# Table products with bf16 one-hots: a token's number as two bf16 parts, in place of one fp32 number

## The chip, the cores and the metric

The kernel runs on one core of one Trainium2 chip. The metric is the device time of one execution in microseconds (us). The engines are named as in the profile: PE (TensorE; PEld is its weight load), DVE (VectorE), ACT (ScalarE), POOL (GpSimd) and SP (SyncE, which here only issues transfers).

## The reference

A state-space scan (Mamba-2's SSD) for 4 batches, 8 heads, 768 steps, head size 32 and state size 16 gives 3072 rows of 256 numbers. A cosine router then sends every row to one of 8 experts, and the expert's two matrices turn the row. What matters here is the routing:

```python
logits = xn @ en.T / tau
expert_idx = np.argmax(logits, axis=1)
...
for e in range(E):
    mask = expert_idx == e
    h = np.maximum(x[mask] @ w1[e], 0.0)
    out[mask] = gate_w[mask, None] * (h @ w2[e])
```

The mask of an expert is, in the kernel, a table: for each expert and each place in it, the number of the token that stands there.

## The kernel before

**The scan.** `mamba` goes through the 768 steps in 6 chunks of 128 steps; a chunk has 4 units of 128 tokens, one per batch. In each chunk PE makes inner products (`inner`, L351), DVE masks them (`mask_inner`, `g`, L361), PE makes the outputs from the running states and the masked products (L372, L389, L402), turns them into rows (`finish`, L421), ACT copies the rows (L413, L430, L432) and SP sends them to a table of rows in DRAM, `y_rows` (`send_rows`, L436). The state goes from chunk to chunk through `decay_states` (`T` on DVE, L307, then `U` on POOL, L313) and `add_sums` (`V` on DVE, L336). `scale_c` makes `cp` on DVE (L243), `pass_c` scales a part of it on POOL (L256), and `scale_first_half` makes `xb` on POOL (L278).

**The routing.** It trails the scan by some chunks, in small steps between the scan's. `pick` (L533 to L539) makes for each token of a chunk a one-hot of its expert (`ob`, bf16). `count_picks` (POOL, L544) keeps running counts of the units. `rank_rows` (PE, L559) gives each token its rank within its expert, by products of bf16 matrices of ones, and ACT copies the ranks (L567). `places` (DVE, L578 to L603) splits a rank into a tile of 104 places and the place within the tile. It makes two one-hots: `eq`, over 8 experts x 4 tiles, and `hot`, over the 104 places. `eq` is multiplied by the token's number plus 1 (`tok1`). `locate` (PE, L613) multiplies the two for each of the 4 units of the chunk, `hot` as the weights and `eq` as the moving operand: the result, 104 places x 32 tiles, holds the number of the token at each place, plus 1.

```python
        k.nc.tensor.matmul(
            k.pz[0][:TR, 424 : 424 + E * NT], lhsT=hot[:, b, :],
            rhs=eq[:].rearrange("p (b e) t -> p b (e t)", b=NB)[:, b], start=(first and b == 0),
```

ACT copies this table out of PSUM (L624) and POOL adds it up (L629).

**Where the calls stand.** The order on each engine is the order of the program; nothing reorders it. `places` of chunks 0, 1, 2 and 3 is called at the end of chunks 2, 3, 4 and 5, that of chunk 4 and 5 in `scan_end`. `locate` of chunks 0 and 1 is called in chunks 3 and 4, ahead of the second half of `finish`; that of chunk 2 in `early_places` in chunk 5, where DVE completes an early table `gi0` (L860, L862) from the first three chunks. With it POOL gathers the first rows of experts 0 and 1 (L876), PE turns them (L970), and the copy of the turned rows (L973) releases held weight loads (L84, L91) and a held send of rows. `locate` of chunks 3, 4 and 5 is called in `scan_end`, between the matmuls of the first expert (L983, L1000). `end_places` (L636 to L646) makes the full table `gi` and the rows of the output. From it come the gathers of all other rows. Those gathers wait for the sends of the last chunks' rows too.

**The experts.** `moe` runs through the 8 experts: `up` (L983), `down` (L1000, or L1045 with fewer products), `out` (L1085 to L1088), with gathers, weight loads and gates (`Gates`) beside them. `moe_end` is the end.

**Constants.** `route_consts` makes the number tables on POOL with `ints`: an iota (L494) and a cast to fp32 (L496) each.

Of the kernel before, what the change touches and what calls it, by code (L numbers as in the profile page):

```python
# [8 lines left out]
F32 = mybir.dt.float32  # L9
I32 = mybir.dt.int32  # L10
BF16 = mybir.dt.bfloat16
ACT = mybir.ActivationFunctionType
ALU = mybir.AluOpType
# [3 lines left out]
NB, NH, S, D, N = 4, 8, 768, 32, 16  # L17
Q = 128
HQ, SQ = Q // 2, Q // 4
NC = S // Q  # L20
NU = NB * NC
T = NB * S
DM, E, F = NH * D, 8, 1024
KD, KF = DM // 128, F // 128
TR, NT = 104, 4
# [23 lines left out]
def load(k, c):  # L49
    nc = k.nc  # L50
    t = k.ld[c]

    def in_(name, shape):
        return k.inp.tile([128] + shape, F32, name=name, tag=name)

    t.ct, t.bi, t.b = in_("ct", [NB, Q]), in_("bi", [NB, Q]), in_("b", [NB, 128])
    t.x, t.xa = in_("x", [NB, DM]), in_("xa", [NB, 128])
    def whole(dst, src):
        nc.sync.dma_start(dst[:].rearrange("p b m -> p (b m)"), src[c])

    whole(t.ct, k.CT)
    if c < 2:
        whole(t.bi, k.BT)
    whole(t.x, k.x)
    nc.sync.dma_start(t.xa[HQ:, :, :], k.x[c, 0:HQ, :].rearrange("p (b m) -> p b m", b=NB)[:, :, 128:])
    whole(t.b, k.B)
    if c >= 2:
        whole(t.bi, k.BT)
# [109 lines left out]
def spread_decays(k, c):  # L178

    for b in range(NB):  # L180
        r = slice(32 * b, 32 * b + 32)
        k.nc.tensor.matmul(
            k.pg[:, b, 384:512], lhsT=k.spread[r, c % 4, :], rhs=k.f[r, c // 4, 0:Q], start=True, stop=True,
            tile_position=(32 * b, 0),
        )
# [144 lines left out]
def add_sums(k, c):  # L330
    for j in range(2):
        s, v = k.pz[j][:, W : W + 128], k.V[:, 2 * j : 2 * j + 2, :].rearrange("p b m -> p (b m)")
        if c == 0:
            k.nc.vector.tensor_copy(out=v, in_=s)
        else:
            k.nc.vector.tensor_tensor(  # L336
                out=v, in0=s, in1=k.ld[c].U[:, 2 * j : 2 * j + 2, :].rearrange("p b m -> p (b m)"), op=ALU.add
            )
# [231 lines left out]
def places(k, c):  # L570


    nc = k.nc
    w = k.work
    be = [128, NB, E]
    u = slice(NB * c, NB * c + NB)
    v = k.at.pop(c)
    nc.vector.scalar_tensor_tensor(  # L578
        out=v[:], in0=v[:], scalar=1.0, in1=k.ob[:, u, :], op0=ALU.add, op1=ALU.mult
    )  # L580
    nc.vector.reduce_sum(out=k.s1[:, u], in_=v[:], axis=AX.X)
    ge = w.tile([128, NB, NT - 1], F32, name="ge", tag="ge")
    nc.vector.tensor_tensor(
        out=ge[:], in0=k.s1[:, u].unsqueeze(2).to_broadcast([128, NB, NT - 1]),
        in1=k.first_of[:, 1:].unsqueeze(1).to_broadcast([128, NB, NT - 1]), op=ALU.is_gt,
    )
    p = w.tile([128, NB], F32, name="pl", tag="pl")
    nc.vector.reduce_sum(out=p[:], in_=ge[:], axis=AX.X)
    nc.vector.scalar_tensor_tensor(
        out=p[:], in0=p[:], scalar=-float(TR), in1=k.s1[:, u], op0=ALU.mult, op1=ALU.add  # L590
    )
    nc.vector.tensor_tensor(out=v[:], in0=v[:], in1=p[:].unsqueeze(2).to_broadcast(be), op=ALU.subtract)
    eq = k.eq[c] = w.tile([128, NB * E, NT], F32, name="eq", tag="eq")
    nc.vector.tensor_tensor(
        out=eq[:], in0=v[:].rearrange("p b e -> p (b e)").unsqueeze(2).to_broadcast([128, NB * E, NT]),
        in1=k.first_of[:].unsqueeze(1).to_broadcast([128, NB * E, NT]), op=ALU.is_equal,
    )
    nc.vector.tensor_tensor(
        out=eq[:].rearrange("p (b e) t -> p b (e t)", b=NB), in0=eq[:].rearrange("p (b e) t -> p b (e t)", b=NB),
        in1=k.tok1[:, c, :].unsqueeze(2).to_broadcast([128, NB, E * NT]), op=ALU.mult,  # L600
    )
    hot = k.hot[c] = w.tile([128, NB, TR], F32, name="hot", tag="hot")
    nc.vector.tensor_tensor(  # L603
        out=hot[:], in0=k.place_at[:].unsqueeze(1).to_broadcast([128, NB, TR]),
        in1=p[:].unsqueeze(2).to_broadcast([128, NB, TR]), op=ALU.is_equal,
    )


def locate(k, c, first=True, last=True):

    eq, hot = k.eq.pop(c), k.hot.pop(c)
    for b in range(NB):
        k.nc.tensor.matmul(  # L613
            k.pz[0][:TR, 424 : 424 + E * NT], lhsT=hot[:, b, :],
            rhs=eq[:].rearrange("p (b e) t -> p b (e t)", b=NB)[:, b], start=(first and b == 0),
            stop=(last and b == NB - 1), skip_group_check=True,
        )


def keep_located(k, c):  # L620
    i = k.idx
    if c > 0:
        i = k.ix = k.work.tile([TR, E * NT], F32, name="ix", tag="ix")
    k.nc.scalar.copy(out=i[:], in_=k.pz[0][:TR, 424 : 424 + E * NT])  # L624
# [24 lines left out]
def mamba(k):  # L649
    nc = k.nc  # L650
# [38 lines left out]
    for c in range(NC):  # L689
        t = k.ld[c]  # L690
        n = c + 1
        if c + 2 < NC:
            load(k, c + 2)
        if 2 <= c < NC - 1:
            spread_decays(k, n)
        if 2 <= c < NC - 1:
            add_sums(k, c)
        if c >= 2:
            inner(k, c, 0)
        if c == NC - 1:  # L700
            early_places(k, c - 3)
        if c >= 2:
            mask_inner(k, c, 0)
        if 3 <= c < NC - 1:
            finish(k, c - 1, (0,))
            locate(k, c - 3)
            keep_located(k, c - 3)
        if n < NC:
            scale_x(k, n, nc.gpsimd)
        if 1 <= c < NC - 1:  # L710
            scale_c(k, n)
        if c == 1:
            add_sums(k, c)
        if c >= 2:
            pick(k, c - 2)
        if c > 0:
            finish(k, c - 1, (1,) if 3 <= c < NC - 1 else (0, 1))
            keep_rows(k, c - 1)
            if c < NC - 1:
                send_rows(k, c - 1)  # L720
        if c == 2:
            spread_ends(k, 1, k.pz[0][:, 400:424])
        inner(k, c, 1)
        mask_inner(k, c, 1)
        if c == NC - 2:
            load_weights(k, 0, (0,), t.masked)
        if c == 0:
            sums(k, 0)
        if n < NC:
            split_b(k, n)  # L730
            mask_c(k, n)
        if c == NC - 1:
            k.early_x = early_rows(k)
            gather_halves(k, k.early_x, k.gi0, 0, 0, 3 * NB * Q)
        if c >= 2:
            count_picks(k, c - 2)
        if c == NC - 1:
            gather_halves(k, k.early_x, k.gi0, 0, 1, 3 * NB * Q)
        if c == 0:
            between(k, n, 4)  # L740
            scale_first_half(k, n, nc.gpsimd, (0,))
        elif n < NC:
            scale_first_half(k, n, nc.gpsimd)
            if c == 3:
                between(k, n, NC)
            pass_c(k, n)
        if 3 <= c < NC - 1:
            add_located(k, c - 3)
        if c > 0:
            from_states(k, c)  # L750
        if 2 <= c < NC - 1:
            rank_rows(k, c - 2)
            keep_ranks(k, c - 2)
        outputs(k, c, 0)
        if c == 0:
            clear_first_half(k, 1)
            spread_decays(k, 2)
            inner(k, 1, 0)
            mask_inner(k, 1, 0)
            add_sums(k, 0)  # L760
        outputs(k, c, 1)
        if c == NC - 1:
            early = early_jobs(k)
            early[0].turn_x()
            rank_rows(k, c - 2)
            keep_ranks(k, c - 2)
        first_outputs(k, c)
        keep_outputs(k, c)
        if c == NC - 1:
            load_weights(k, 0, (1,), early[0].turned)  # L770
            hold(k, send_rows(k, c - 1), early[0].turned)
            load_weights(k, 1, (0,), early[0].turned)
            early[0].w2, early[1].w1 = k.w2t[0], k.w1t[1]
        if c + 2 < NC:
            sums(k, n)
        if c == 2:
            turn_inverses(k, 1, k.pz[0][:, 0:256])
        if c == NC - 1:
            pick(k, c - 1)
            count_picks(k, c - 1)  # L780
        if c >= 2:
            places(k, c - 2)
        if c == 4:
            shift_places(k)
        if c == 1:
            decays(k, 1)
            block_ends(k, 1)
            inverses(k, 1)
        if n < NC:
            decay_states(k, n)  # L790
        if c == 0:
            scale_first_half(k, n, nc.gpsimd, (1,))
            pass_c(k, n)
# [72 lines left out]
def early_rows(k):  # L866
    return k.ep.tile([TR, 2 * HT, KD * Y1], F32, name="xg", tag="xg", bufs=2)
# [602 lines left out]
```

## Time and profile before

| what | value |
| --- | --- |
| median of 4 runs | 272.74 us (271.85, 272.13, 273.34, 273.42) |
| the profiled execution | 273.11 us |
| its span, first to last instruction | 271.4 us |
| mean granted PE clock | 0.983 |
| PE busy | 255.8 us (94%) |
| POOL busy | 159.1 us (59%) |
| DVE busy | 149.7 us (55%) |
| ACT busy | 70.9 us (26%) |
| DMA | 35.87 MB, mean 132 GB/s |

The profiled execution took 1.7 us more than its span. Shares of busy time are means over stages that differ: the scan ends near 75 us, and the experts run from there on. A line of a group reads: line, engine, operation, tiles written and read, shapes, count, then busy time in all and mean ns of one, and then the idle time in front of them with what ended it. A line of the time line reads: start, length, engine, line, operation, tiles, shapes, count, and in brackets the idle time in front. A line of the stretches reads: the stretch, its length, the busy time of PE, PEld, DVE, ACT and POOL, the granted PE clock, the share of the DMA engines and GB/s.

### The profile page before, as it was taken

How to read it: one execution, taken by the hardware profiler on the slowest of the kernel's cores; microseconds unless marked ns; L12 is line 12 of the kernel's file. 1: busy time of each engine (PE TensorE's matmuls, PEld its weight loads, DVE VectorE, ACT ScalarE, POOL GpSimd, SP SyncE). 2: the span in 40 equal slices, each digit the busy share in tenths (PEclk: the TensorE clock that was granted, in tenths of full speed). 3: DMA queues.
4: the chain of work that ended last, by engine and by line, in shares of the span. 5: the costliest groups of instructions: out<-in, count | busy, mean ns of one | idle time of the engine just before them, and what ended most of it. 6: DMA issues, size and time to landing. Idle time of an engine off the chain costs nothing.

```text
span 271.4 us, 6221 instructions
## 1 busy us (share of the span) xinstructions
PE 255.8 (94%) x2446; PEld 208.4 (77%) x2446; DVE 149.7 (55%) x396; ACT 70.9 (26%) x216; POOL 159.1 (59%) x193
## 2 busy tenths in 40 slices
PE   7989799999999989999999999999999999999990
PEld 2677688888899979997589569659857956975890
DVE  6686875898754103245564466468458546733021
ACT  2714515343461415131320231131032023101000
POOL 8999454764413805479468768758956975005022
PEclk9999959999999999999999999999999999999998
DMA  3968763337499951989446418527521101002011
GB/s 118 329 222 254 208 211 90 121 99 164 111 289 299 224 156 40 213 240 221 122 100 149 151 56 188 166 60 168 168 77 38 49 18 38 1 0 64 5 31 31
DMA packets 22303, 35.87 MB, mean 132 GB/s; under 512 B 2547, under 2 KB 15550, under 8 KB 22272
## 3 DMA queue, kind: packets, MB, share of 16 engines
q1 hardware_dynamic: 19024, 28.73, 38.3%
q0 software_dynamic: 3072, 6.67, 9.7%
q8 instruction: 20, 0.33, 0.5%
q14 instruction: 11, 0.09, 0.1%
q10 hardware_dynamic: 176, 0.06, 0.1%
HBM read 29.05 MB, written 6.65 MB: 132 GB/s over the span
## 4 chain that ended last, share of the span: by engine, by line
PE 47%; issue 14%; DMA 13%; POOL 13%; DVE 9%; ACT 1%; POOLq 1%; SPq 0%; DVEq 0%
PE hp L983 22%; PE yp L1045 13%; DMA xg<-y_rows,gi 5%; DMA out_dram<-yo,to 4%; DMA w<-in_moe_w_dram 4%; POOL xb L278 3%; DVE g L361 3%; PE yp L1000 2%; POOL xg L876 2%; POOL out_dram L1088 2%; PE pg L351 2%; POOL spread L110 1%; PE ot L1085 1%; PE eb L1000 1%; PE py L402 1%
## 5 line engine op out<-in xcount | busy, mean ns | idle before, releaser
L983 PE MATMUL hp<-xT,w 128*128 128x416 f32 (+1 forms) x256 | 83.9, 469 | 0.0
L1088 POOL DMA_INDIRECT out_dram<-yo,to x32 | 34.5, 1079 | 55.3 <-DVE yo L1087 53.8
L983 PEld LDWEIGHTS hp<-xT,w 128*128 128x128 f32 x256 | 45.8, 190 | 21.6 <-issue 21.6
L876 POOL DMA_INDIRECT xg<-y_rows,gi x32 | 43.8, 1370 | 16.5 <-issue 7.3
L987 ACT ACTIVATE hT<-hp 128x416 f32<-128x416 f32 (+1 forms) x32 | 15.2, 474 | 81.8 <-PE hp L983 81.7
L989 DVE TENSOR_SCALAR hT<-hp 128x416 f32<-128x416 f32 (+1 forms) x32 | 17.2, 536 | 29.6 <-PE hp L983 29.6
L361 DVE TENSOR_TENSOR g<-pg,mask 128x1536 f32<-128x1536 f32 x12 | 21.1, 1754 | 7.4 <-PE pg L351 7.4
L1000 PE MATMUL yp<-hT,w 128*128 128x208 f32 x128 | 23.4, 340 | 0.3 <-PEq L1302 0.3
L1000 PEld LDWEIGHTS yp<-hT,w 128*128 128x128 f32 x128 | 22.3, 190 | 0.9 <-issue 0.9
L1045 PE MATMUL yp<-T,S 128*128 128x208 f32 x120 | 22.7, 339 | 0.0
L1045 PEld LDWEIGHTS yp<-T,S 128*128 128x128 f32 x120 | 21.2, 190 | 0.0
L1115 POOL TENSOR_TENSOR gr<-gr,half 104x4 f32<-104x4 f32 x8 | 8.7, 1090 | 14.1 <-ACT sq L1109 14.0
L1045 PE MATMUL yp<-hT,w 128*128 128x208 f32 x80 | 16.1, 344 | 0.2 <-ACT p L1061 0.2
L1045 PEld LDWEIGHTS yp<-hT,w 128*128 128x128 f32 x80 | 13.7, 190 | 1.0 <-ACT p L1061 0.9
L1109 ACT ACTIVATE sq<-xg 104x256 f32<-104x256 f32 x32 | 13.0, 407 | 0.0
L983 PE MATMUL eb<-xT,w 128*128 128x208 f32 x64 | 12.8, 345 | 0.0
L1020 POOL TENSOR_TENSOR S<-w 128x512 f32<-128x512 f32 x10 | 12.7, 1268 | 0.1
L265 POOL TENSOR_TENSOR xs<-x,rT 128x1024 f32<-128x1024 f32 x6 | 11.8, 1968 | 0.9 <-ACT rT L223 0.8
L1000 PE MATMUL eb<-hT,w 128*128 128x208 f32 x64 | 12.0, 341 | 0.0
L544 POOL TENSOR_TENSOR pre<-pre,ob 128x8 bf16<-128x8 bf16 x24 | 4.8, 200 | 12.1 <-DVE ob L539 10.7
L351 PE MATMUL pg<-cp,bi 32*128 32x128 f32 x192 | 11.4, 311 | 0.0
L1087 DVE TENSOR_SCALAR yo<-yp,gate 104x256 f32<-104x256 f32 x12 | 5.8, 483 | 9.7 <-PE yp L1085 9.7
(224 smaller groups left out, 430.6 us busy)
## 6 DMA issues: line engine op xcount, KB each, us to landing
w<-in_moe_w_dram SPq DMA_DIRECT2D x16, 512.0 KB, 6.8
w<-in_moe_w_dram SPq DMA_DIRECT2D x8, 1024.0 KB, 6.8
y_rows<-rows SPq DMA_DIRECT2D x6, 528.0 KB, 4.4
x<-in_x_dram SPq DMA_DIRECT2D x6, 512.0 KB, 5.4
ct<-in_CT_dram SPq DMA_DIRECT2D x6, 256.0 KB, 4.9
bi<-in_BT_dram SPq DMA_DIRECT2D x6, 256.0 KB, 3.0
b<-in_B_dram SPq DMA_DIRECT2D x6, 256.0 KB, 5.2
xa<-in_x_dram SPq DMA_DIRECT2D x6, 128.0 KB, 5.4
```

Of the source, the lines that this page charges most:

```text
L265: engine.tensor_tensor(out=t.xs[:].rearrange("p b (h d) -> p b h d", h=NH), in0=t.x[:].rearrange("p b (h d) -> p b h d", h=NH), in1=r_of(k ...
L351: k.nc.tensor.matmul(k.pg[:, q, 192 * u + a : 192 * u + a + n], lhsT=m, rhs=x, start=True, stop=True, tile_position=(32 * q, 0),)
L361: t.masked = k.nc.vector.tensor_tensor(out=g[:], in0=k.pg[:, :, 0:384].rearrange("p q (u m) -> p q u m", u=2), in1=k.mask[:].unsqueeze(1). ...
L876: k.nc.gpsimd.indirect_dma_start(out=x, out_offset=None, in_=k.y_d[0:rows, :], in_offset=bass.IndirectOffsetOnAxis(ap=at, axis=0), bounds_ ...
L983: nc.tensor.matmul(t, lhsT=s.w1[:, j, 128 * f : 128 * f + 128], rhs=s.xT[:, j, :], start=(j == 0), stop=(j == KD - 1))
L987: nc.scalar.activation(s.hT[:, f, :], t, ACT.Relu)
L989: nc.vector.tensor_scalar_max(s.hT[:, f, :], t, 0.0)
L1000: nc.tensor.matmul(t, lhsT=s.w2[:, f, 128 * j : 128 * j + 128], rhs=s.hT[:, f, r], start=(f == 0), stop=(f == KF - 1))
L1020: k.nc.gpsimd.tensor_tensor(out=s.S[:, n], in0=x, in1=y, op=op)
L1045: nc.tensor.matmul(t, lhsT=a[:, f], rhs=b[:, f], start=start and f == 0, stop=(f == 3), skip_group_check=True)
L1088: d = nc.gpsimd.indirect_dma_start(out=k.out[:, :], out_offset=bass.IndirectOffsetOnAxis(ap=s.to[:, i : i + 1], axis=0), in_=y[:], in_offs ...
L1109: s.k.nc.scalar.activation(sq[:], s.x[:, i, :].rearrange("p (j w) -> p j w", j=KD)[:, :, 0:128], ACT.Square, accum_out=s.r[:, i : i + 1],)
```

## The change

The token's number plus 1 was one fp32 number, multiplied into `eq`. Now it is the sum of two numbers: the token's row in its unit plus 1 (1 to 128, `row1`), and the first number of its unit (a multiple of 128 up to 2944, `unit_at`). Each of the two is exact in bf16. `eq` becomes a bf16 tile with two halves, one multiplied by each number, and `hot` becomes bf16. `locate` makes two bf16 products for each unit in place of one fp32 product, into the same fp32 sum in PSUM. `places` has one DVE instruction more. The two number tables are made in chunk 1, on POOL between `scale_first_half` and `pass_c`.

```diff
-    eq = k.eq[c] = w.tile([128, NB * E, NT], F32, name="eq", tag="eq")
+
+    eq = k.eq[c] = w.tile([128, 2, NB * E, NT], BF16, name="eq", tag="eq")
     nc.vector.tensor_tensor(
-        out=eq[:], in0=v[:].rearrange("p b e -> p (b e)").unsqueeze(2).to_broadcast([128, NB * E, NT]),
+        out=eq[:, 0], in0=v[:].rearrange("p b e -> p (b e)").unsqueeze(2).to_broadcast([128, NB * E, NT]),
         in1=k.first_of[:].unsqueeze(1).to_broadcast([128, NB * E, NT]), op=ALU.is_equal,
     )
     nc.vector.tensor_tensor(
-        out=eq[:].rearrange("p (b e) t -> p b (e t)", b=NB), in0=eq[:].rearrange("p (b e) t -> p b (e t)", b=NB),
-        in1=k.tok1[:, c, :].unsqueeze(2).to_broadcast([128, NB, E * NT]), op=ALU.mult,
-    )
-    hot = k.hot[c] = w.tile([128, NB, TR], F32, name="hot", tag="hot")
+        out=eq[:, 1].rearrange("p (b e) t -> p b (e t)", b=NB),
+        in0=eq[:, 0].rearrange("p (b e) t -> p b (e t)", b=NB),
+        in1=k.unit_at[:, c, :].unsqueeze(2).to_broadcast([128, NB, E * NT]), op=ALU.mult,
+    )
+    nc.vector.tensor_scalar(out=eq[:, 0], in0=eq[:, 0], scalar1=k.row1[:], scalar2=None, op0=ALU.mult)
+    hot = k.hot[c] = w.tile([128, NB, TR], BF16, name="hot", tag="hot")
...
     for b in range(NB):
-        k.nc.tensor.matmul(
-            k.pz[0][:TR, 424 : 424 + E * NT], lhsT=hot[:, b, :],
-            rhs=eq[:].rearrange("p (b e) t -> p b (e t)", b=NB)[:, b], start=(first and b == 0),
-            stop=(last and b == NB - 1), skip_group_check=True,
-        )
+        for i in range(2):
+            k.nc.tensor.matmul(
+                k.pz[0][:TR, 424 : 424 + E * NT], lhsT=hot[:, b, :],
+                rhs=eq[:, i].rearrange("p (b e) t -> p b (e t)", b=NB)[:, b], start=(first and b == 0 and i == 0),
+                stop=(last and b == NB - 1 and i == 1), skip_group_check=True,
+            )
...
-            if c == 3:
+            if c == 1:
+                k.row1 = k.ints("row1", [128, 1], [[0, 1]], 1, 1)
+                k.unit_at = k.ints("unit_at", [128, NC, NB], [[NB * Q, NC], [Q, NB]], 0, 0)
+            elif c == 3:
                 between(k, n, NC)
```

## The prediction

> **What bounds the kernel now.** I read the page first, then stretches of busy time, the groups, the time lines of TensorE (PE), VectorE (DVE) and GpSimd (POOL) between 30 and 100 us, and the chain of waits. All `locate` calls lie between 43.9 and 85 us, so only that part can be touched directly. From the page:
>
> ```profile
> PE 255.8 (94%) x2446; PEld 208.4 (77%) x2446; DVE 149.7 (55%) x396; ACT 70.9 (26%) x216; POOL 159.1 (59%) x193
> PEclk9999959999999999999999999999999999999998
> ```
>
> PE fills the span, and in one slice it had half its clock. The same in stretches (PE busy first, PEclk after POOL):
>
> ```profile
> 29.80:33.20 3.40, 2.08 (x15) 1.59 (x13) 2.67 (x5) 2.08 (x7) 2.54 (x2) 1.00 0.62 130
> 33.20:36.60 3.40, 3.23 (x56) 3.01 (x60) 2.04 (x7) 1.34 (x4) 1.90 (x6) 0.51 0.03 10
> 94.60:98.05 3.45, 2.38 (x16) 2.09 (x15) 0.00 (x0) 0.33 (x1) 0.88 (x5) 1.00 1.07 276
> ```
>
> After 1.3 us of idle PE in 3.4 us (2.08 busy) the clock was halved, and it stayed so to 40.0; after 1.07 us of idle (2.38 of 3.45 busy) it was not. I come back to this.
>
> The groups, and PE's time line where two chunks are located in one go, beside the ranking products, which are bf16 already:
>
> ```profile
> L613 PEld LDWEIGHTS pz<-eq,hot 128*104 128x104 f32 x48 | 5.0, 171 | 0.6 <-DVE hot L603 0.6
> L613 PE MATMUL pz<-eq,hot 128*104 128x32 f32 x48 | 5.0, 251 | 0.4 <-DVE hot L603 0.4
> L559 PEld LDWEIGHTS <-ones_b 128*128 128x128 bf16 x9 | 0.7, 99 | 0.2
> ```
> ```profile
> 76.22 1.57 PE L613 MATMUL pz<-eq,hot 128*104 128x32 f32 x16
> 78.42 0.18 PE L559 MATMUL pz<-ob,before_b 128*128 128x32 bf16 x1
> 78.47 0.22 PE L559 MATMUL pz<-ob,ones_b 128*128 128x24 bf16 x3
> ```
>
> The 24 fp32 products appear as 48 loads and 48 matmuls: each product is two pairs. A pair takes (1.57 - 0.25) / 15 = 0.088 us, a bf16 pair of 128 columns (0.22 - 0.17) / 2 = 0.025 us.
>
> DVE and POOL in chunk 3, where `places` of chunk 1 runs:
>
> ```profile
> 49.20 0.64 DVE L578 SCALAR_TENSOR_TENSOR rk<-rk,ob 128x32 f32<-128x32 f32 x1
> 50.92 0.59 DVE L594 TENSOR_TENSOR eq<-rk,first_of 128x128 f32<-128x128 f32 x1
> 51.55 0.29 DVE L598 TENSOR_TENSOR eq<-eq,tok 128x128 f32<-128x128 f32 x1
> 51.76 0.58 DVE L603 TENSOR_TENSOR hot<-place_at,pl 128x416 f32<-128x416 f32 x1
> 52.26 0.42 DVE L307 TENSOR_TENSOR T<-V,wm 128x256 f32<-128x256 f32 x1
> ```
> ```profile
> 48.71 1.08 POOL L278 TENSOR_TENSOR xb<-xa,rT 64x512 f32<-64x512 f32 x1
> ...
> 50.73 0.63 POOL L256 TENSOR_TENSOR cp<-cp,ends 128x256 f32<-128x256 f32 x1
> 52.76 0.62 POOL L313 TENSOR_TENSOR U<-T,ends 128x256 f32<-128x256 f32 x1 [1.39 <-DVE T L307]
> ```
>
> L578 ends at 49.84, when POOL's 48.71 instruction ends (49.79); L594 ends at 51.51, just after POOL's 50.73 one (51.36). Their free durations are 0.19 and 0.29. So here DVE waits for POOL, and then POOL for DVE (1.39 us idle until T). The chain T, U, V, g is what moves chunk 4 on, not PE.
>
> The chain of waits, 60 to 104 us (start, length, what):
>
> ```profile
> 64.36 1.30 POOL xg L876
> ...
> 65.96 3.77 DMA xg<-y_rows,gi
> ...
> 69.78 0.49 PE eb L970 x3
> ...
> 88.28 9.41 DMA xg<-y_rows,gi
> ...
> 97.74 0.49 PE eb L970 x3
> ```
>
> The first gather starts when the early table (`gi0`, L862) is ready at 64.02; PE's transposes and, behind them, the held weight loads follow it. The second gather starts at 86.83 though its table `gi` was ready at 85.21, so a transfer released it. The chain names a weight load, which the gather does not wait for in the program; the sends of rows, behind weights on the same queue, are what it waits for. PE is then idle until the rows land at 97.74. From there PE is full to the end. Hence the time moves by what `gi0` moves, and PE saved between 70 and 97 only lengthens the wait at 97.7.
>
> **The change, part by part.**
>
> *TensorE.* 24 fp32 products (48 pairs) become 48 bf16 products (48 pairs): the number of loads stays. What a bf16 load of 104 columns costs no row shows. Upper bound: today's 0.088; lower bound: the ranking's 0.025. That the load sets the pace, and not the moving columns, is seen in L201: four fp32 pairs of 128 columns with only 12 moving take 0.61 us at 32.11, or (0.61 - 0.26) / 3 = 0.117 each, more than L613 with 104 and 32. I take 0.088, the row of the same width and tile; then only the last product's length changes, 0.25 to about 0.18, so -0.07 per chunk. With 0.025 a chunk of 8 pairs saves 7 x 0.063 + 0.07 = 0.51 us.
>
> The Trainium skill ("TensorE: Matmul & The Clock Gate", section on weight-path perf modes) says that the fast weight load is on when there are 128 weights and the type is not fp32; `hot` has 104. That rule speaks against this change; with it no load gets shorter, without it PE would do 48 x 0.063 = 3.0 us less work. No run so far shows a bf16 load of 104.
>
> *DVE.* The two `eq` instructions keep their elements and their duration: L539 writes bf16 in 192 ns as its fp32 neighbours do. `hot` still reads fp32, 0.58. New is one multiplication per call, 128x128 bf16 in place. Six calls. By start to start it costs at least 0.21 (L598 to L603, no wait between) and at most 0.33 (L594 to L598 where free, 39.41 to 39.74); beside a POOL instruction up to 0.64, as L578. I take 0.25, because POOL is idle when it comes (51.4 to 52.8 and 61.3 to 64.4). Behind it on DVE stand `hot`, T, and in chunk 4 the early table.
> - Call of chunk 0 (at 40): T comes 0.25 later, U ends at 41.8 instead of 41.57; V waits until 42.36 for L223 anyway. Covered by 0.5; cost 0, without the cover 0.25.
> - Call of chunk 1 (at 51.8): nothing covers it. T, U, V and all of chunk 4 move: +0.25. The shorter end of `locate` in chunks 3 and 4 gives nothing: L578 waits for POOL until 49.84 whenever it starts after 48.71, and chunk 4's inner products wait for `cp` on DVE.
> - Call of chunk 2 (at 62): +0.25 on `hot`, for which PE waits already (0.38 idle before L613 at 62.59). The table's addition L860 at 63.62 waits for the end of `locate` (63.51); T ends at 63.42. So -0.07 there with slow loads, -0.18 at most with fast ones, when T becomes the last.
> - Calls of chunks 3, 4, 5 (72.6, 74.9, 80.7): `pick` and the last ranking move by 0.5, but L559 at 78.42 has ob since 76.65, and the last `hot` at 81.53 waits for PE until 83.9. Covered; gi has 1.6 us to spare. Cost 0.
>
> *POOL.* Two iotas and two casts in chunk 1, ahead of L256 at 26.78. The pairs for `rank` and `tok` took 8.73 to 9.53, 0.8 in all for both. POOL is then idle for 2.52 us (until 29.92), which covers them; without that, 0.8. But L256 now runs at 27.5 to 28.2 beside DVE's small decay instructions (27.71 on), which feed T at 29.48, so by the stalls above up to 0.36. Half of a delay there is lost again at 40.0, when the clock comes back at its own time. Bounds 0 and 0.36; I take 0.15.
>
> *Sum.* 0.25 + 0.25 + 0.15 - 0.07 = +0.6 us. The profiled execution took 273.11, so 273.7; it stands 0.37 above the median of 272.74 of the runs, so 273.3 for the median. With the low ends, 0.21 + 0.21 + 0 - 0.18 = +0.2; with the free high ends, 0.33 + 0.33 + 0.36 = +1.0. A measurement of this kernel tells about 0.5%, 1.36 us, from no change.
>
> **Rivals.**
>
> *DVE stalls (slower).* The added instruction meets POOL and takes 0.64 in chunks 3 and 4, as L578 and L594 do, and the POOL pairs cost 0.36: 1.6 us, and 0.14 more at chunk 0 when its 0.5 of cover is passed: +1.7, or 274.5. For: half the stretched rows are this kind. Against: POOL waits for DVE just then. It decides once the instruction starts while POOL still runs L256 (before 51.36).
>
> *The clock (much slower).* With pairs of 0.025, PE saves 23 x 0.063 = 1.45 us in the locates at 76.2 and 83.9. The gather is not earlier, so PE is idle for 1.07 + 1.45 = 2.5 us before 97.7. That is more than the 1.3 which halved the clock at 33.2. A halved clock of 6.8 us, as there, costs 3.4 us of PE where PE is full: with the 0.6, +4.0, or 276.7. It decides above about 1.3 us of idle in one stretch of 3.4, and needs the fast loads.
>
> The skill's same page has the clock fall only after a whole idle window of about 3.4 us; here it fell after 1.3 idle in 3.4. By the page this rival would cost nothing.
>
> *PE sets the pace (faster).* PE is 89 to 100% busy in chunks 3 to 5. If loads are fast and the stalled DVE rows only follow PE (L578 slips in before 48.71), three locates give 3 x 0.51 = 1.5: with DVE's additions hidden, 271.2. Against: POOL's idle time until T.
>
> *The change doesn't do what it says:* slow loads leave PE as it was; that is inside my forecast.
>
> **How the numbers follow.** Forecast 0.45 (own range 272.4 to 274.1), DVE stalls 0.22, clock 0.11, PE sets the pace 0.15, something not seen 0.07. The four times before fall into two pairs 1.3 us apart, so neighbours blur. Of the forecast 0.07 lies above 274.1, of the stalls 0.04 below it; the unseen part is shared out as 0.02 faster, 0.02 same and 0.03 slower. Slower 0.07 + 0.18 + 0.11 + 0.03 = 0.39, same 0.38 + 0.04 + 0.02 = 0.44, faster 0.15 + 0.02 = 0.17. The range 271.6 to 275.0 takes in the forecast and the stalls and leaves out the clock and most of the faster case.
>
> **What would show it.** Right: 48 loads of `hot` near 0.088 apart (0.025 brings the clock and PE cases in); the added instruction at 0.17 to 0.29 us, not 0.6; T of chunk 1 a quarter later after its POOL instruction; the first gather 0.4 to 0.8 later than 64.36 and the rows at 97.7 later by as much. Wrong: a second half-clock stretch near 98, `gi0` earlier than 64.0, or a time that moves by over 1.4 us while `gi0` does not.

## The result, and the profile after

The changed kernel took 272.79 us (median of 44 runs, 270.97 to 275.01); the kernel before 271.73 us (median of 70, 269.39 to 275.12). The ratio is 1.0042, 95% interval [1.0027, 1.0058], so the change costs about 1.15 us. That is inside the 0.5% that was called no change, and inside the range; the forecast had +0.6. The interval leaves out 1, so a small cost is there.

The profiled execution of the changed kernel took 270.91 us. It happened to be a quick one, 2.2 us below the profiled execution of before. Its page shows why. The rows of busy time and of the granted clock:

```profile
PE 251.4 (93%) x2446; PEld 203.9 (76%) x2446; DVE 151.5 (56%) x402; ACT 70.7 (26%) x216; POOL 159.7 (59%) x197
PEclk9999999999999999999999999999999999999996
```

The slice with half the clock (33.2 to 40.0 in the profile of before) is missing. So the two profiles must not be subtracted at absolute times: everything after 50 us comes about 2.1 us earlier here. Whether the change had a part in that is taken up with the tables alone, below. PE's instruction count is the same as before (2446), DVE has six more, POOL four more.

The groups of the touched lines (busy us, mean ns of one, idle time before them), and PE's time line at the double locate that stood at 76.22 with 1.57 us:

```profile
L617 PE MATMUL pz<-eq,hot 128*104 128x32 bf16 x48 | 3.0, 198 | 0.8 <-DVE hot L606 0.7
L617 PEld LDWEIGHTS <-hot 128*104 128x104 bf16 x48 | 3.0, 128 | 1.2 <-DVE hot L606 0.9 <-issue 0.3
```
```profile
74.00 0.90 PE L617 MATMUL pz<-eq,hot 128*104 128x32 bf16 x16
81.05 0.52 PE L617 MATMUL pz<-eq,hot 128*104 128x32 bf16 x8
```

A pair takes (0.90 - 0.20) / 15 = 0.047 us. That is neither the 0.088 that the forecast took nor the 0.025 of its lower bound. Sixteen pairs are 0.67 us shorter than before and eight 0.31, so PE has 0.98 us less to do between 70 and 97 us.

POOL in the second chunk, where the two tables are made (start, length):

```profile
26.78 0.14 POOL L494 IOTA row_i<- 128x1 int32 x1
26.99 0.32 POOL L496 CAST row<-row_i 128x1 f32<-128x1 int32 x1
27.26 0.19 POOL L494 IOTA unit_at_i<- 128x24 int32 x1
27.52 0.21 POOL L496 CAST unit_at<-unit_at_i 128x24 f32<-128x24 int32 x1
27.69 0.62 POOL L256 TENSOR_TENSOR cp<-cp,ends 128x256 f32<-128x256 f32 x1
29.73 0.62 POOL L313 TENSOR_TENSOR U<-T,ends 128x256 f32<-128x256 f32 x1 [1.43 <-DVE T L307]
```

L256 starts 0.91 later than before (26.78), POOL still waits 1.43 us for T afterwards, and U starts at 29.73 where it started at 29.92 before. The cover held, and more than that: U is 0.19 earlier. On DVE, L165, which stands ahead of T on its queue, starts at this time. First the profile of before, where L256 runs from 26.78 to 27.40, then this one:

```profile
26.89 0.78 DVE L165 TENSOR_TENSOR_SCAN f<-a,heads 128x128 f32<-128x128 f32 x1
```
```profile
26.90 0.42 DVE L165 TENSOR_TENSOR_SCAN f<-a,heads 128x128 f32<-128x128 f32 x1
```

It took 0.78 in all five profiles of kernels without the tables, and 0.42 in all nine with them. L175, which now starts beside L256, takes 0.38 where it took 0.22, so about half of this gain of 0.36 is left.

DVE with the added instruction (L604) in chunk 3, and the V that its T leads to:

```profile
48.90 0.29 DVE L599 TENSOR_TENSOR eq<-eq,unit_at 128x128 bf16<-128x128 bf16 x1
49.22 0.49 DVE L604 TENSOR_SCALAR eq<-eq,row 128x128 bf16<-128x128 bf16 x1
49.64 0.58 DVE L606 TENSOR_TENSOR hot<-place_at,pl 128x416 bf16<-128x416 f32 x1
50.14 0.41 DVE L307 TENSOR_TENSOR T<-V,wm 128x256 f32<-128x256 f32 x1
51.28 0.49 DVE L336 TENSOR_TENSOR V<-pz,U 128x128 f32<-128x128 f32 x2 [0.73 <-POOL U L313]
```

Here it met POOL's L256 (49.01 to 49.67) and took 0.49; in the other five calls it took 0.25 or 0.26.

Then the end of the touched part, in PE's time line (idle time before it in brackets). The profile of before had here:

```profile
97.74 0.49 PE L970 MATMUL eb<-ident,xg 104*128 104x104 f32 x3 [1.07 <-DMA xg<-y_rows,gi]
```

The changed kernel:

```profile
90.41 2.98 PE L1007 MATMUL eb<-hT,w 128*128 128x208 f32 x16
94.99 0.31 PE L977 MATMUL eb<-ident,xg 104*128 104x104 f32 x1 [1.61 <-DMA xg<-y_rows,gi]
95.60 0.49 PE L977 MATMUL eb<-ident,xg 104*128 104x104 f32 x3 [0.30 <-DMA xg<-y_rows,gi]
```

PE waits 1.91 us for the late rows, where it waited 1.07 before: what the locates save is idle time here, as the prediction said. From these second transposes to the end of the span it is 269.2 - 95.6 = 173.6 us, and in the profile of before 271.4 - 97.74 = 173.7. So in these two profiles the landing of the late rows sets the time; what can come on top is a lower clock of PE behind it.

### The profile page after: what moved, and what is told of

It reads as the page before. It is cut to its first block, busy times and chain, and to the rows that moved or that the text cites. A ratio compares the mean times of both kernels' runs of the same rounds, so it can differ in the third digit from the quotient of the medians.

```text
span 269.2 us, 6229 instructions
## 1 busy us (share of the span) xinstructions
PE 251.4 (93%) x2446; PEld 203.9 (76%) x2446; DVE 151.5 (56%) x402; ACT 70.7 (26%) x216; POOL 159.7 (59%) x197
## 4 chain that ended last, share of the span: by engine, by line
PE 45%; POOL 16%; issue 15%; DMA 12%; DVE 10%; POOLq 1%; ACT 1%; SPq 0%; DVEq 0%
PE hp L990 22%; PE yp L1052 13%; DMA out_dram<-yo,to 5%; DMA w<-in_moe_w_dram 4%; POOL xb L278 4%; DMA xg<-y_rows,gi 4%; DVE g L361 2%; PE yp L1007 2%; POOL out_dram L1095 2%; POOL xs L265 1%; POOL spread L110 1%; POOL xg L883 1%; PE ot L1092 1%; PE eb L1007 1%; POOL U L313 1%
## 5 line engine op out<-in xcount | busy, mean ns | idle before, releaser
L1007 PEld LDWEIGHTS eb<-hT,w 128*128 128x128 f32 x64 | 11.1, 190 | 0.0
```

The source lines that it names most:

```text
L1007: nc.tensor.matmul(t, lhsT=s.w2[:, f, 128 * j : 128 * j + 128], rhs=s.hT[:, f, r], start=(f == 0), stop=(f == KF - 1))
```

## The experiments

Each was timed in five rounds beside the kernel before on the same chip, four kernels to a chip. Three theories of the +1.15 us were set against each other: D, VectorE's added instruction; P, the tables on GpSimd; C, the clock, halved by PE's longer wait for the late rows. W, that PE's saving is lost in that wait, joined them later. One measure, called the piece below, is read from every trace: the time from the start of the first V of chunk 1 (30.38 after) over the next two V (40.86, 51.28) to the first gather (62.24), which is 31.86 us in the changed kernel. "Issue" in a bracket is time in which an engine waited for nothing that the profile shows.

**The tables alone** (the kernel before, with the change's lines in the loop over chunks).

```
+            if c == 1:
+                k.row1 = k.ints("row1", [128, 1], [[0, 1]], 1, 1)
+                k.unit_at = k.ints("unit_at", [128, NC, NB], [[NB * Q, NC], [Q, NB]], 0, 0)
```

> The kernel before, with the two number tables of the change (two iotas, two casts) made by GpSimd in chunk 1 and then not used. Measured for the whole change: +1.15 us. Three theories for these. D, VectorE's added instruction: 0.29 us per call start to start in the trace after, 0.53 where it met GpSimd, in the calls of chunks 3 and 4 that nothing covers, so some 0.5 to 0.8 of the 1.15; this kernel, which lacks it, then stands within 0.2 of the kernel before. P, the tables: they hold up the decay chain of the next chunk by up to 0.4 and so the whole pipeline; this kernel then takes 0.3 to 0.4 more, or up to 1.1 if P is all of it. C, the clock: the shorter locate leaves TensorE idle for longer before the late rows, a half-clock stretch comes in more of the executions; nothing of that here, so 0. I expect D: 0 to +0.2, with T of that chunk within 0.1 of its place before.

Measured: 273.08 against 272.35, ratio 1.0010 [0.9980, 1.0041]; over the runs with a mean clock of at least 0.989 the medians are 272.22 and 272.12. T of that chunk came at 29.87 here, but V of the chunk before stood at 20.86 and g at 24.13 already, 0.6 late before the tables. In the change and with the multiplication on ScalarE, both with tables, the first V stands at 30.38 and 30.37; without tables at 30.57 (before) and 30.60 (the next experiment). So P has no row to stand on as a cost: where nothing else is late, the tables bring the first V 0.2 us forward. With PE at full clock the measured piece is 10.21 + 10.33 + 10.96 = 31.50 us: this is the reference for the next ones. It is the kernel before with the tables; no profile of the kernel before as it is has this piece at full clock. The clock rows of the four profiles that have neither the tables nor the added instruction (before; with the move; with the longer wait; with the unused products; the last three come further down):

```profile
PEclk9999959999999999999999999999999999999998
PEclk9999959999999999999999999999999999999998
PEclk9999979999999999999999999999999999999997
PEclk9869979999999999999999999999999999999998
```

All four have a half clock in the sixth slice, for 6.8, 6.8, 3.4 and 3.4 us, and their piece is 33.79, 33.73, 32.45 and 32.32 us. None of the nine profiles with the tables has it, nor has the next experiment's, which lacks them. So the tables, by the earlier V, may keep PE's clock up there in some executions. That would be a gain of the change, and the three theories leave it out. No run tests it, and one profile of each kernel can't show how often it comes.

DVE's time line of the tables-alone kernel in chunk 3:

```profile
49.21 0.29 DVE L598 TENSOR_TENSOR eq<-eq,tok 128x128 f32<-128x128 f32 x1
49.42 1.01 DVE L603 TENSOR_TENSOR hot<-place_at,pl 128x416 f32<-128x416 f32 x1
50.35 0.41 DVE L307 TENSOR_TENSOR T<-V,wm 128x256 f32<-128x256 f32 x1
51.50 0.49 DVE L336 TENSOR_TENSOR V<-pz,U 128x128 f32<-128x128 f32 x2 [0.73 <-POOL U L313]
```

Without the added instruction it is `hot` that meets L256 and takes 1.01 in place of 0.58. The added instruction takes over this stall, so in that chunk it costs only 0.09.

**The instruction alone** (the kernel before, with one more multiplication in each call).

```
+    more = w.tile([128, NB * E, NT], BF16, name="more", tag="more")
+    nc.vector.tensor_scalar(out=more[:], in0=eq[:], scalar1=k.half[:, 0:1], scalar2=None, op0=ALU.mult)
     hot = k.hot[c] = w.tile([128, NB, TR], F32, name="hot", tag="hot")
```

> The kernel before (fp32 tables, fp32 products) with one more VectorE instruction in every places call: a 128x128 multiplication by a scalar ahead of hot, written in bf16 to a tile that nobody reads. D: +0.5 to +0.8 as in the change, for it stands ahead of hot, T and the early table in chunks 3 and 4; it reads fp32 and writes elsewhere, so 0.05 to 0.1 us longer or shorter than the change's own. P: 0, no tables here. C: 0, the locate has the length of before. If the time stays within 0.2 of before, D falls.

Measured: 273.25 against 272.35, ratio 1.0027 [1.0005, 1.0049], or +0.74 us. The piece is 10.52 + 10.47 + 11.28 = 32.27, so +0.31, +0.14 and +0.32 against the tables alone: +0.77. D holds for the instruction by itself, where nothing pays it back. This kernel has no tables, so the reference differs from it in two things. In the change the same three are 10.48, 10.42 and 10.96: +0.27, +0.09 and 0.00, together +0.36. The third is paid back by the shorter locate (0.31), behind which the early table stands. The piece starts at the first V, so the 0.19 that the tables gain ahead of it is not in it: against the kernel before at full clock, the first gather of the changed kernel is an estimated 0.36 - 0.19 = 0.17 us late.

**The multiplication on ScalarE** (the changed kernel, in place).

```
-    nc.vector.tensor_scalar(out=eq[:, 0], in0=eq[:, 0], scalar1=k.row1[:], scalar2=None, op0=ALU.mult)
+    nc.scalar.activation(eq[:, 0], eq[:, 0], ACT.Copy, scale=k.row1[:])
```

> The changed kernel with the added multiplication given to ScalarE (Copy with a scale of one number per partition, same tile) in place of VectorE. VectorE's queue is then as long as before, and the locate's halves wait for ScalarE, beside hot (0.58). D: the 0.5 to 0.8 goes, so -0.1 to +0.4 against the kernel before, and hot of the call of chunk 1 starts 0.2 to 0.3 after L599, not 0.5 to 0.8. P and C: it stays where the change is, +1.0 to +1.3. If ScalarE is late (it is 26% busy), the locate waits for it and the gain is smaller.

Measured: 273.12 against 272.35, ratio 1.0010 [0.9982, 1.0037]: the interval holds both D's and P's number. The trace says more: 10.19, 10.32 and 11.59. In the first two chunks the cost is gone, in the third it is 0.63, since the locate waits for ScalarE (0.30), whose instruction takes 0.41. Its sum is +0.60, more than on VectorE.

**Weights of 128 columns** (the changed kernel; zeros in the 24 more, filled once).

```
-    hot = k.hot[c] = w.tile([128, NB, TR], BF16, name="hot", tag="hot")
+    hot = k.hot[c] = k.wide[c % 2]
...
-                k.pz[0][:TR, 424 : 424 + E * NT], lhsT=hot[:, b, :],
+                k.pz[0][:, 424 : 424 + E * NT], lhsT=hot[:, b, :],
```

> The changed kernel with 128 weight columns in every locate product in place of 104: the 24 more are zeros, written once by GpSimd behind the tables (two tiles, so two fills more in chunk 1). It tells what the width does to a bf16 pair (0.048 us with 104 in the trace after, 0.025 for the ranking's 128) and what PE time in the locate is worth. D: PE does not set the pace there, so the time is that of the change within 0.2 (+1.0 to +1.3), P: plus up to 0.3 for the fills. C: the pairs get shorter by 0.02, the idle time before the late rows longer by 23 x 0.02 = 0.5, so more half-clock stretches: 0.3 to 1.5 above the change, and a lower mean clock in the runs. PE sets the pace: 0.2 to 0.5 below the change. I expect 0.025 a pair and the time of the change.

Measured: 273.87 against 272.35, ratio 1.0056 [1.0021, 1.0091]. Its last locate in PE's time line, and its loads in the groups:

```profile
84.58 0.35 PE L617 MATMUL pz<-eq,hot 128*128 128x32 bf16 x8
```
```profile
L617 PEld LDWEIGHTS <-hot 128*128 128x128 bf16 x48 | 1.9, 96 | 1.4 <-DVE hot L606 1.1 <-issue 0.2
```

A pair takes (0.35 - 0.18) / 7 = 0.025 us: loading more columns is quicker, 96 ns in place of 128. PE's time fell once more and the kernel did not get faster, so "PE sets the pace" has nothing to stand on (over the runs with a mean clock of at least 0.989 the medians are 273.11 and, before, 272.12). 7 of its 12 runs had a mean clock under 0.989, but that does not show C: in the kept profile (0.974) the half clock lies at 12.8 to 23.0, long before any locate, and the clock stayed up around the late rows.

**The changed kernel again**, for a second profile.

> The changed kernel as it is, for a second profile and its times beside the next three on one chip. By the first experiments the piece from the first V (GpSimd's sum added) to the first gather takes 31.50 us without the added instruction (tables alone), 31.86 in the change, and the end follows the last landing of the late rows by 173.6. D (the added instruction): 31.7 to 32.0 here again, with the chunk from the second to the third V 0.2 to 0.3 over the 10.21 of tables alone; +0.4 to +0.8 against the kernel before. C (clock): mean clocks of the runs below those of the kernel before, with more of them under 0.99 (54% of the first runs were; before: 31% on this chip), and the difference in time between runs of a clock over 0.99 under 0.3. If the piece is 31.5, D falls.

Measured: 273.20 against 271.38 on this chip, ratio 1.0047 [1.0014, 1.0080]. The piece is 31.87 again, so D's part repeats to 0.01 us. What differs is the clock. In all the traces the stretches between two changes of the granted clock are whole multiples of 3.41 us (half clocks of 3.41, 6.83 and 10.24), so the borders of its windows can be counted from one change. PE's time line, and the stretches cut at these borders (after the engines' busy times, the granted clock):

```profile
90.70 2.98 PE L1007 MATMUL eb<-hT,w 128*128 128x208 f32 x16
95.61 0.31 PE L977 MATMUL eb<-ident,xg 104*128 104x104 f32 x1 [1.93 <-DMA xg<-y_rows,gi]
96.21 0.52 PE L977 MATMUL eb<-ident,xg 104*128 104x104 f32 x3 [0.30 <-DMA xg<-y_rows,gi]
96.53 4.68 PE L1007 MATMUL eb<-hT,w 128*128 128x208 f32 x16
```
```profile
93.07:96.49 3.42, 1.20 (x8) 0.70 (x7) 0.00 (x0) 0.33 (x1) 0.60 (x4) 1.00 1.08 262
96.49:99.90 3.41, 3.41 (x13) 3.33 (x12) 0.00 (x0) 0.51 (x1) 0.00 (x0) 0.51 0.32 105
```

Both parts of the wait fell into one window, PE was busy for 1.20 of 3.42 us, and in the next 3.41 us it had half its clock: sixteen products took 4.68 us, in the first profile 3.00. That costs 3.41 / 2 = 1.7 us. The sum closes for this pair of profiles: from the first profile of the changed kernel (269.2) the rows land 0.61 later (0.51 of it is a wait of PE on issue at 66 us), and 269.2 + 0.61 + 1.7 = 271.5, the span here. In that first profile the wait was nearly as long (1.91 us, here 2.23), but a border cut it in two. Its stretches:

```profile
90.89:94.30 3.41, 2.50 (x15) 2.17 (x13) 0.00 (x0) 0.39 (x2) 2.02 (x6) 1.00 1.09 235
94.30:97.71 3.41, 2.42 (x15) 2.25 (x16) 0.00 (x0) 0.51 (x1) 0.00 (x0) 1.00 0.84 238
```

Such a half window lowers the mean clock of an execution by about 0.006. A mean clock of 0.985 to 0.988 was found in 28 of the 58 executions of the changed kernel (18 of 46 and 10 of 12) and in 15 of 105 of the kernel before on three chips. On the chip of this experiment alone it is 10 of 12 against 6 of 35. The mean does not say where in an execution the half clock lay.

**The wait filled with work that is due anyway.** The second expert's last product is cut, and five of its eight steps go ahead of the transposes; once in the kernel before, once in the changed one, same chip.

```
     second.down(0)
+    second.down(1, fs=range(5))
     late[0].turn_x()
-    second.down(1)
+    second.down(1, fs=range(5, KF))
```

> The kernel before, with five of the eight contraction steps of the second expert's last product moved ahead of the transposes of the late rows: 1.9 us of work that needs nothing from the late gather, put where TensorE is idle for 1.0 to 1.4 us. Theory W (TensorE's time saved between 70 and 97 us is lost in this wait): here the wait falls to 0 and the time by 0.5 to 1.3, and TensorE becomes what sets the end. If the late rows are what the end follows whatever PE does in between, the time is that of before within 0.2. Rows that land early would now wait for 1.9 us of products, without loss, since those are due anyway.

> The changed kernel with the same move. W: the changed kernel has the longer wait there (1.9 us in its profile, 1.1 before), so it gains 0.5 to 0.8 more by the move than the kernel before does, and stands level with the kernel before with the move, or 0.3 below; against the kernel before -0.5 to -1.5. D alone: the added instruction's 0.4 to 0.8 stays, and this one stands as far above the other as the change did without the move. C: the idle time ahead of the late rows is gone and with it the half-clock stretches after it; the mean clocks come up to those of the kernel before.

Measured: the kernel before with the move 270.05, ratio 0.9936 [0.9907, 0.9965]; the changed kernel with it 269.59, ratio 0.9919 [0.9882, 0.9956]; the kernel before 271.38 and the changed one 273.20 on this chip. The move gives the one 1.3 us and the other 3.6. PE's time line of the changed kernel with the move, and a stretch around that wait:

```profile
95.10 0.26 PE L978 MATMUL eb<-ident,xg 104*128 104x104 f32 x1
95.68 0.49 PE L978 MATMUL eb<-ident,xg 104*128 104x104 f32 x3 [0.33 <-DMA xg<-y_rows,gi]
```
```profile
93.07:96.49 3.42, 3.09 (x20) 2.80 (x19) 0.00 (x0) 0.61 (x2) 0.41 (x3) 1.00 1.04 265
```

The wait is down to 0.33, and none of its 12 runs has a mean clock between 0.985 and 0.988 (10 of 12 without the move). With the wait covered the change stands 0.46 us below the kernel before, in medians; the two intervals overlap, so level is what is shown. No part of the +1.15 is seen. This is what W and C say; the move covers a later landing of the rows too, so D's 0.36 can't be seen there.

**The move, and the multiplication beside VectorE.** ScalarE reads the one-hots from a tile of their own and no longer waits for the other half.

```
+    e1 = w.tile([128, NB * E, NT], BF16, name="e1", tag="e1")
...
+    nc.scalar.activation(eq[:, 0], e1[:], ACT.Copy, scale=k.row1[:])
...
-    nc.vector.tensor_scalar(out=eq[:, 0], in0=eq[:, 0], scalar1=k.row1[:], scalar2=None, op0=ALU.mult)
```

> The changed kernel with that move, and with the added multiplication on ScalarE, which now reads the one-hots from a tile of their own and so starts while VectorE makes the other half (in the first try on ScalarE it came after it, in place, and the locate of the fifth chunk waited for it: 0.63 there). D: the piece from first V to first gather is 31.50 or less: 10.2 and 10.3 for two chunks as without the added instruction, and 10.96 less up to 0.3 for the shorter locate in the third, so 0.4 to 0.7 below the changed kernel with the move; the fastest of all, -1 to -2 against the kernel before. P or C: level with the changed kernel with the move.

Measured: 269.64, ratio 0.9926 [0.9892, 0.9959]: level with the changed kernel with the move. The expectation of 0.4 to 0.7 less fell. The piece is 10.18 + 10.37 + 11.54 = 32.09: in the third chunk ScalarE is still late, for another reason. Its time line there:

```profile
59.68 1.07 ACT L413 COPY yT<-py 128x512 f32<-128x512 f32 x2 [3.32 <-PE py L402]
60.64 0.41 ACT L600 ACTIVATE eq<-e,row 128x128 bf16<-128x128 bf16 x1
```

The one-hots are ready at 59.22, but two copies stand ahead of L600 on that queue. A queue that is 26% busy was occupied just then.

**ScalarE in the first two calls only**, with the move.

> The changed kernel with the last product's five steps ahead of the late rows, and with the added multiplication on ScalarE in the calls of chunks 0 and 1 alone; the others keep it on VectorE, since the call of chunk 2 waited for ScalarE by 0.30 in both tries. From first V to first gather: 10.2 + 10.35 + 10.95 = 31.5, as with tables alone, 0.35 below the change. Time: 0.0 to 0.4 below the changed kernel with the move (269.59 on its chip, 1.79 below the kernel before there): -1.8 to -2.2 against the kernel before. If the gather no longer sets the pace there, because TensorE is full once its wait is covered, level with that kernel.

Measured: the piece is 10.20 + 10.37 + 10.91 = 31.48, as expected. The time is 271.90 against 272.75 on another chip, ratio 0.9971 [0.9937, 1.0005]: a gain in the first gather that the time does not show, and 1.8 to 2.2 less was expected. Whether it is worth anything stays open; this profile has 1.8 us of PE waits on issue after that gather.

**The wait filled with products that nobody reads**, in the changed kernel and, as a control, in the kernel before.

```
     second.down(0)
+    bank = k.next_bank()
+    for i in range(4):
+        k.nc.tensor.matmul(bank[:], lhsT=k.warm[:, 0:Q], rhs=k.warm[:], start=True, stop=True)
     late[0].turn_x()
```

> The changed kernel with four products of 512 columns (bf16 ones, result unused, 0.85 us at full clock) ahead of the transposes of the late rows: TensorE is busy for part of its wait there and nothing useful moves. In the second profile of the changed kernel the wait was 1.93 + 0.30 us within one window of the clock gate (busy 1.20 of 3.42) and the clock then stood at half for 3.4 us; 10 of 12 runs had a mean clock of 0.986 or 0.987. C: the wait falls to about 1.1, the window stays above the share at which it trips (1.44 idle did not trip it, 2.22 did), most runs come to a clock over 0.99, and the time falls from +1.3 to within 0.3 of the kernel before. W without C: the rows land when they did, so the time stays at +1.0 to +1.5; where they land early the dummies cost up to 0.85.

> The control: the same four unused products in the kernel before, whose wait there is 1.1 to 1.4 us. C: within 0.3 of before, or 0.3 below if some of its low-clock runs come from this window; where the rows land early the dummies cost up to 0.85. It bounds what the products themselves cost.

Measured: the changed kernel with them 273.29, ratio 1.0021 [0.9989, 1.0054]; the kernel before with them 272.94, ratio 1.0004 [0.9971, 1.0036]; before 272.75. In the changed kernel the share of mean clocks from 0.985 to 0.988 fell from 28 in 58 to 2 in 12, and the two kernels differ by 0.35 us in place of 1.15. The products had their price where the rows came early: over the runs of at least 0.989 the medians are 272.50 and 272.75 against 271.95. So nothing useful moved, PE's idle time fell, and most of the difference went with it. This points to C; the two intervals overlap and the chips differ, so it does not show it alone. The kept profile (0.978) has its half clock at 13.0 to 23.2; around the late rows PE waited for 1.14 us and the clock stayed up.

**A longer wait in the kernel before**: two fills of 0.53 us on GpSimd between the first and the second late gather, with the fp32 locate as it was.

> The kernel before, with two fills of 128x512 (0.53 us each) on GpSimd between the first and the second late gather: the second rows land 1.06 to 1.2 us later, and TensorE is idle there for 2.1 to 2.5 us in place of 1.1 to 1.4, with the fp32 locate unchanged. C: the longer idle time alone trips the clock in most runs: mean clocks of 0.986 as in the changed kernel, and +1.1 for the delay plus up to 1.7 for the 3.4 us at half clock, +2.0 to +2.9 in the median. Without C (the half clocks of the changed kernel come from something else in it): +0.8 to +1.2 and clocks as in the kernel before.

Measured: 274.27 against 272.75, ratio 1.0053 [1.0023, 1.0084]; the medians differ by 1.52, between the two expectations. The mean clock lay between 0.985 and 0.988 in 6 of 12 runs (5 of 35 for the kernel before on this chip). It does not settle C: in its profile (0.988) the half clock was the one of the sixth slice, at 33.9 to 37.3. At the late rows PE was late by its own waits, the idle time was 1.44 us and the clock stayed up.

## Why the prediction was right or wrong, point by point

The number held: +0.6 forecast, +1.15 [0.7, 1.6] measured, both under the 1.36 us that the forecast called no change. It held in part by luck: the term for TensorE was mis-sized, terms for VectorE and GpSimd erred in both directions, and a rival was at work that the forecast left out. The 272.74 that it was built on is 1.0 above the median of the 70 runs.

- **TensorE, the mis-sized term.** "I take 0.088" was too much: a pair took 0.047 us with 104 bf16 columns, 0.025 with 128. The row of the same width and the row of the same type each had half of the answer. The locate of eight pairs is 0.31 shorter, not 0.07. The Trainium skill ("TensorE: Matmul & The Clock Gate", section on weight-path perf modes) asks for 128 weights and a type other than fp32; the runs agree that the 128 columns are quicker than the 104, and show besides that bf16 with 104 is well below fp32 with 104, so leaving the rule unmet did not mean no gain.
- **DVE.** 0.25 for the instruction was right, 0.29 from start to start. Its places were not. "Covered by 0.5; cost 0" in chunk 2 failed: +0.27. The cover came from PE at half clock in that profile (V waiting until 42.36, and until 42.31 in the one with the move); in the changed kernel, at full clock, V follows T by 1.15 and there is none. "+0.25" in chunk 3 was 0.09, since the instruction takes over a stall of `hot`. In chunk 4, +0.18 was 0.00, since the locate is shorter than it was taken for. The sum, 0.43, came out near 0.36 by errors that cancel.
- **POOL.** 0.15 taken, 0 to 0.36 as bounds; the sign was wrong. The forecast looked for DVE instructions that would meet the later L256, and not for the one that ran beside L256 all along: L165 got 0.36 shorter, and the first V comes 0.19 earlier. The tables alone stand at a ratio of 1.0010.
- **The gathers.** The first gather moves by +0.36 from the first V, by an estimated +0.17 with the earlier V (forecast 0.6). That rows, not the table, release the second is borne out: SyncE sends the last rows at 75.42 before, 73.19 after and 73.49 in the second profile, and the gather follows by 11.41, 11.39 and 11.53, though its table was ready 1.6 to 2.7 us earlier. "PE saved between 70 and 97 only lengthens the wait" is what the move of the product showed.
- **The clock, the rival with 0.11.** Its mechanism was the right one, its condition and its price were not. It was tied to pairs of 0.025; 0.047 and an idle time of 2.2 in one window were enough. Its bound of 1.3 us of idle in 3.4 fell: 1.44 left the clock up (with ScalarE's multiplication). It was priced at 6.8 us of half clock, as at 33.2; it was 3.4, so 1.7 us. And it does not come or stay away, it comes in a part of the executions, in the two profiles by where the window's border fell. (0.48 - 0.14) x 1.7 = 0.6 us is an estimate of its mean cost from the counts above, and with D's 0.17 to 0.36 it makes 0.8 to 1.0 of the 1.15. The sum isn't closed: the counts by mean clock hold other half-clock stretches too, and clocks under 0.985 are rarer in the changed kernel (7 of 58 against 22 of 105), as they would be if the tables kept the clock up in the sixth slice.
- **The clock's rule.** The same page of the skill (Part 1, on the clock gate) lets the clock fall after an idle window of about 3.4 us. The length of the half clock agrees (3.41 us). Read as a wholly idle window, as the prediction did, it does not agree: the clock fell with PE busy for 1.20 of 3.42.
- **DVE stalls, 0.22.** The stall came once in six calls (0.49), where it replaced another one. The first gather moved by 0.36 and not by 1.7.
- **PE sets the pace, 0.15.** Ruled out by the 128 columns: quicker pairs, no gain. Whether it comes true once the wait for the rows is covered is not shown: the 0.46 us there are within the noise.
- **Its own signs.** Two of the three signs of being wrong came. `gi0` was ready at 61.90, earlier than 64.0, because this profile lacks the half clock at 33; and the second profile has a half clock behind the late rows, at 96.5. The pairs were not near 0.088 either.

The lowest ratio of the study is that of the changed kernel with five steps of the product ahead of the transposes (0.9919 of before). Most of that comes from the move, which the kernel before can have as well (0.9936, level within the noise).

## What to carry to other kernels

Time saved on an engine ahead of a wait goes into the wait, and on TensorE a longer wait can also cost the clock of the work behind it: look for work that is due anyway and put it into the wait before the stage is made quicker. A cover that is read from one profile has to be checked for what made it: here it was a half clock at 33 to 40 us that no profile of the changed kernel has. An instruction that is put on one engine can also shift what another engine meets, for the better as well as for the worse. Compare two kernels over intervals between the same events, not at absolute times, and place a cost beside what it displaces, a stall or a later wait.

## What the runs showed of the hardware that was not expected

What halves the clock is not PE's busy share alone. With ScalarE's multiplication the window ahead of the late rows had PE busy for 1.97 of 3.41 us and the clock stayed; in the profile of before 2.08 of 3.40 at 29.8 lowered it. Those had products of 12 columns among them (L201). At that place, in windows cut at the borders, the clock fell with PE busy for 2.06 to 2.33 us (the four profiles with the half clock in the sixth slice) and stayed with 2.43 in the changed kernel's first profile. What is counted was not found out.

PE also waits on nothing that the profile shows, by amounts that differ from one execution to the next. In the tables-alone kernel:

```profile
66.17 0.65 PE L372 MATMUL py<-cp,T 32*64 32x128 f32 x11 [0.36 <-issue]
68.11 0.28 PE L389 MATMUL py<-g,xs 128*32 128x64 f32 x3 [0.40 <-issue]
68.83 0.32 PE L389 MATMUL py<-g,xs 128*32 128x64 f32 x5 [0.45 <-issue]
69.57 0.46 PE L389 MATMUL py<-g,xs 128*32 128x64 f32 x14 [0.41 <-issue]
```

The last three come 0.7 us apart while the first gathers are under way. There the last rows were sent 13.24 us after the first gather, against 10.95 in the first profile of the changed kernel, which has no such wait. That is up to 2 us of scatter in the kernel's time; its cause was not tried.
